# Attention and GEGLU block on one core: a raw copy for half products, dense loads placed after the last sums' store, and two-step cycles from step 24

## The chip, the cores and the metric

The kernel runs on 1 core of one Trainium2 chip. The metric is device time in microseconds (us) of that core, the median of several runs; lower is better. Engines are named as the profile names them: PE is TensorE's matmuls and PEld its weight loads, DVE is VectorE, ACT is ScalarE, POOL is GpSimd, SP is SyncE, which here only issues DMAs. A queue of DMAs belongs to the engine that issues them, and an engine issues them in its program order.

## The reference

One transformer block on 2048 tokens of width 512: attention with 32 query heads of 16 elements over one shared key and value head, then a GEGLU feed-forward layer of width 1792. Both have a layer norm ahead and a residual behind.

```python
def _A_ref(x, wq, wk, wv, wo):
    q = split_heads(x @ wq)            # 32 heads of 16
    k, v = x @ wk, x @ wv              # shared by all heads
    p = softmax((q @ k.T) * 16 ** -0.5)
    return merge_heads(p @ v) @ wo

def _B_ref(x, w_gate, w_up, w_down):
    return (gelu(x @ w_gate) * (x @ w_up)) @ w_down

h = x + _A_ref(layernorm(x), wq, wk, wv, wo)
out = h + _B_ref(layernorm(h), w_gate, w_up, w_down)
```

## The kernel before

**Tiling.** The tokens are cut into four query blocks b of 512 (`NB`, `T`). Attention goes block by block, in each block through eight groups g of four heads (`NG`), in each group through 16 chunks of 128 keys (`KC`). One step n is one key chunk for two of the four heads: two matmuls of scores into a tile `s` (L394), and one exponential of 128x1024 by ACT from `s` to `p` (L398). Two steps make a chunk, a group is 32 steps, a block 256. When a chunk's `p` is there, `weigh` multiplies it with the values and adds into the PSUM bank `acc` (L402). Chunks that are scored and not yet weighed stand in the list `pend`, and `finish(k)` weighs the oldest k of them. With a group's last chunk `evacuate` copies `acc` to `oT` (DVE, L415), stores it in DRAM as `acc_d` (SP, L419), reads it back re-ordered as `oc` (SP, L428), inverts the sums (L442), multiplies (L445) and splits the result in a high and a low part `o_hi` and `o_lo` (L453, L457). Two groups share one `oc`. When a block's groups are done, the output projection `pp` (L590), layer norm and feed-forward layer of that block (`dense(b)`, matmuls of L913 and L590) are woven into the scores of the next block.

**Products in two parts.** Matmul operands are split into a high and a low part, and a product is three matmuls per 128 rows (high x high, high x low, low x high). The query projection `pq` of a block is four such products, c = 0 to 3 (`project_q`). Its first products run whole (L204). From block 1, c = 2 on they are half products (L392): each matmul takes 64 of the 128 rows of the array, and a score matmul takes the other 64 at the same time. Such a matmul is a token that the generator yields; the loop over n hands tokens to `scores`. When a half product is complete, DVE splits it from its bank into `qh` and `ql` (L119, L120), squares `qh` to `qs` (L1091), and SP stores three parts into `q_d` (L245). After c = 3 the generator yields `REST` for a cycle without tokens, then the matmuls `pqn` (L256) add up the squares of the block's four products, and DVE and POOL make a bound for the softmax from it (`qn`, `mm`, `m`). All `pq` and `pqn` of this stage use one PSUM bank: the pool has one buffer (`width = 1`), and the next product starts when the bank's last reader is done. For three of the whole products, listed in `HURRY`, DVE or ACT copies the bank to a tile `pq_raw` first and the split reads that.

**The first block's loop.** It has two parts. The first, `while n < 2 * KC`, advances whole products at the steps of `RAMP` and then at every fourth step, until the generator yields 0 (`said`), and calls `finish(len(pend) - 2)` at every fourth step: the order on PE is four steps of scores, then two weighings. The second, `while n < lead`, runs cycles of two steps, weighs one chunk per cycle when more than two are pending, and gives out up to four tokens per cycle, later two (`count`). In between it calls `next(parts)`: that loads a piece of the dense weights on SP (L497), splits it on POOL, and stores it to DRAM from POOL's queue (L508, L514). `age()` counts down to the softmax bound's steps. At n = 256 the buffers of this phase are released and POOL loads the output weights `wo` (L564). Four steps later `dense(0)` is started, which issues the loads of two `xb` tiles (L624) and four `w` tiles (L550) on SP. At n = 272 the first block's output projection begins.

**The order.** PE, POOL, ACT, and from the first loop on SP and DVE, run exactly in the order in which the code records instructions. The attention code stands a second time in the program, in a branch that these inputs do not take.

Of the kernel before, what the change touches and what calls it, by code (L numbers as in the profile page):

```python
# [40 lines left out]
HURRY = ((0, 3), (1, 0), (1, 1))  # L41
# [11 lines left out]
def kernel(  # L53
# [26 lines left out]
    KC = S // P  # L80
# [77 lines left out]
    def run(outer, first):  # L158
# [28 lines left out]
        def project_q(b, cs, eng, col, whole=None):  # L187
            halves = whole is not None
            whole = whole if halves else cs
            tsl = slice(b * T, (b + 1) * T)  # L190
            xT_hi, xT_lo = xT[b]
            urgent = b == 0 and cs[0] == 0
            qss = []
            for c in cs:
                pq = psum1(f"pq_{b}_{c}")
                terms = [
                    (wt[:, d, c * P : (c + 1) * P], xt[:, d, :])
                    for d in range(DC)
                    for wt, xt in ((wq_hi, xT_hi), (wq_hi, xT_lo), (wq_lo, xT_hi))
                ]  # L200
                last = len(terms) - 1
                full = c in whole
                for n, (lhsT, rhs) in enumerate(terms if full else ()):
                    nc.tensor.matmul(pq, lhsT, rhs, start=(n == 0), stop=(n == last))  # L204
                    if n % 3 == 2 and (urgent or n < last):
                        yield 3
                for a in range(2) if not full else ():
                    if a:
                        mark = eb.tile([P, 1], F32, tag="qmark", bufs=2, name=f"mark_{b}_{c}")
                        nc.vector.tensor_copy(mark, pq[:, :1])  # L210
                    rows = slice(64 * a, 64 * a + 64)
                    for n, (lhsT, rhs) in enumerate(terms):
                        yield a, last - n, partial(
                            nc.tensor.matmul, pq, lhsT[rows], rhs[rows],
                            start=(a == 0 and n == 0), stop=(a == 1 and n == last),
                            skip_group_check=True,
                        )

                raw = None
                if (b, c) in HURRY:  # L220
                    raw = eb.tile([P, T], F32, tag="vT", bufs=3, name=f"pq_raw_{b}_{c}")
                    if b == 0:
                        nc.scalar.activation(raw, pq, AF.Copy)
                    else:
                        nc.vector.tensor_copy(raw, pq)
                    yield 3
                qh = eb.tile([P, T], F32R, tag="qh", bufs=2, name=f"qh_{b}_{c}")
                ql = eb.tile([P, T], F32R, tag="ql", bufs=2, name=f"ql_{b}_{c}")
                if raw is not None:
                    split(nc.vector, qh, ql, raw)  # L230
                else:

                    split(nc.vector if b == 0 and c == FIRST_Q else eng, qh, ql, pq)
                qs = eb.tile([P, T], BF16, tag="qs", bufs=DC, name=f"qs_{b}_{c}")
                square = partial(
                    (nc.gpsimd if urgent else nc.vector).tensor_tensor,
                    qs, qh.bitcast(F32), qh.bitcast(F32), op=ALU.mult,
                )
                if full:
                    square()  # L240
                else:
                    squares.append(square)
                qss.append(qs)
                for r0, part in ((0, qh), (DH, ql), (2 * DH, qh)):
                    nc.sync.dma_start(  # L245
                        q_d[c * HC : (c + 1) * HC, r0 : r0 + DH, tsl].bitcast(F32),
                        part.bitcast(F32),
                    )
                if not halves and (raw is None or b == 0):
                    yield 3  # L250

            if halves:
                yield REST
            pn = psum1(f"pqn_{b}_{cs[0]}")[:H, :]
            for i, c in enumerate(cs):
                nc.tensor.matmul(  # L256
                    pn, sel[:, c, :], qss[i], start=(i == 0), stop=(i == len(cs) - 1)
                )
            qn = eb.tile([H, T], F32, tag="qn", bufs=1, name=f"qn_{b}_{cs[0]}")
            nc.vector.tensor_copy(qn, pn)  # L260
            nc.vector.tensor_reduce(q2[:, col : col + 1], qn, axis=AX.X, op=ALU.max)

            mm = eb.tile([H, 3], F32, tag="mm", bufs=2, name=f"mm_{b}_{cs[0]}")

            def factors():
                nc.gpsimd.tensor_scalar(
                    mm[:, 0:1], q2[:, col : col + 1], k2m, 1e-30, op0=ALU.mult, op1=ALU.add
                )
                nc.gpsimd.tensor_tensor(
                    mm[:, 1:2], mm[:, 0:1], power[:H, 0:1], op=ALU.pow  # L270
                )
                nc.gpsimd.tensor_scalar(
                    mm[:, 2:3], mm[:, 0:1], mm[:, 1:2], 0.5, op0=ALU.mult, op1=ALU.mult
                )
                nc.gpsimd.tensor_scalar(
                    mm[:, 1:2], mm[:, 1:2], k2m, 0.5, op0=ALU.mult, op1=ALU.mult
                )

            m = eb.tile([H, T], F32R, tag="m", bufs=2, name=f"m_{b}_{cs[0]}")

            def bound():
                nc.vector.tensor_scalar(
                    m, qn, mm[:, 1:2], mm[:, 2:3], op0=ALU.mult, op1=ALU.add
                )
                hs = slice(cs[0] * HC, (cs[-1] + 1) * HC)
                nc.sync.dma_start(q_d[hs, 3 * DH, tsl].bitcast(F32), m[hs].bitcast(F32))

            if urgent:
                yield 2
                factors()  # L290
                nc.scalar.activation(
                    m, qn, AF.Identity, bias=mm[:, 2:3], scale=mm[:, 1:2]
                )
                ms[b] = m
                return
            after.extend([[2, factors], [4, bound]])
            if not halves:
                yield 2
# [680 lines left out]
        PER = NG * KC  # L979
# [58 lines left out]
        with tc.manual_schedule(engines={mybir.EngineType.SP, mybir.EngineType.DVE}):  # L1038
# [2 lines left out]
                work = later_q()  # L1041
                parts = part_weights(early.enter_context(tc.tile_pool(name="parts", bufs=1)))

            while n < 2 * KC:
                for _ in range(RAMP.get(n, n > 7 and n % 4 == 3) if said else 0):
                    said = next(work)
                    age()
                score(n)
                n += 1
                if n % 4 == 0:  # L1050
                    finish(len(pend) - 2)
                    if parts is not None and n > 12 and n % 24:
                        next(parts)

            token, left = next(work) if first else None, 6 * (NB * DC - 2 - DC) * DC
            while n < lead:
                age()
                rest = token == REST
                count = 0
                if token is not None and not rest:  # L1060
                    count = min(4 if left > LAST_Q - n else 2, token[1] + 1)
                    left -= count
                if n == 2 * PER:
                    assert token is None
                    while after:
                        age()
                    for _ in parts or ():
                        pass
                    if first:
                        check_bound(eb, k2m)  # L1070
                    parts = work = None
                    early.close()
                    db = late.enter_context(tc.tile_pool(name="dense", bufs=1))
                    load_wo(0)
                for j in range(2):
                    if j >= 2 - count // 2:
                        tokens = token, next(work)
                        score(n, [(lane, step) for lane, _, step in tokens])
                        token = next(work, None)
                    else:  # L1080
                        score(n)
                    n += 1
                if n == 2 * PER + 4:
                    primed = dense(0)
                    next(primed)
                if rest:
                    token = next(work, None)
                if len(pend) > 2:
                    finish(1)
                while squares:  # L1090
                    squares.pop(0)()  # L1091
                if outs and n % 4 == 0:
                    take_out()
                if parts is not None and n // 2 % 5 in (0, 2):
                    next(parts, None)
# [23 lines left out]
        for c in range(LEAD[0], (NB - 1) * NG * len(SIZES)):  # L1119
# [18 lines left out]
            due, said = 0, None  # L1138
# [380 lines left out]
```

## Time and profile before

| | before |
|---|---|
| median of 3 runs | 1426.1 us (1425.7 to 1427.6) |
| the profiled execution, its own time | 1426.9 us |
| its span, first to last instruction | 1425.1 us |
| PE busy | 1402.1 us, 98% |
| ACT busy | 1045.1 us, 73% |
| DVE busy | 541.8 us, 38% |
| POOL busy | 200.1 us, 14% |
| DMA | 193.69 MB, mean 136 GB/s |

Busy time of PE is a sum over matmuls whose ends are modelled, so 98% does not say that PE works at its peak. A row of the timeline has start, length, engine, line, operation, output<-input with shapes, and in brackets the idle time of that engine just before it, with what ended it. A row of the chain of waits has start, length and what the program's end depended on there. In rows of waits the three numbers are microseconds in total, how often, and the longest.

### The profile page before, as it was taken

What the parts mean: (1) busy time and instruction counts of PE and PEld (TensorE: products, weight loads), DVE (VectorE), ACT (ScalarE), POOL (GpSimd) and SP (SyncE); (2) the same over time, 40 slices, a digit from 0 to 9 for tenths busy, and PEclk for the clock granted to TensorE, in tenths of its full rate; (3) what the DMA queues carried; (4) which work ended last, traced back from release to release, by engine and by line L of the source; (5) the groups of instructions that cost most, each with busy time, mean ns of one, the idle gap of its engine ahead of it and who ended that gap; (6) DMA issues with size and microseconds to landing.
All of it is one profiled execution on the core that took longest, in us unless ns stands there. A gap on an engine that the chain in (4) does not pass through costs nothing.

```text
span 1425.1 us, 25577 instructions
## 1 busy us (share of the span) xinstructions
PE 1402.1 (98%) x10622; PEld 777.5 (55%) x10622; DVE 541.8 (38%) x974; ACT 1045.1 (73%) x1149; POOL 200.1 (14%) x286
## 2 busy tenths in 40 slices
PE   8999999998999999999999999999999999999998
PEld 7533333324555555555555555555555555557886
DVE  7412221213352342424352342423443342427665
ACT  7699999995787787877787777777778777772000
POOL 6365666620000000000000000000000000002000
PEclk9999999999999999999999999999999999999999
DMA  4467776761243241304242242223243241435551
GB/s 158 162 210 264 237 251 230 247 212 48 85 138 109 86 145 61 112 29 176 102 153 93 88 143 72 99 82 124 84 147 115 86 146 34 143 125 193 183 200 62
DMA packets 84700, 193.69 MB, mean 136 GB/s; under 512 B 9676, under 2 KB 24012, under 8 KB 84544
## 3 DMA queue, kind: packets, MB, share of 16 engines
q1 hardware_dynamic: 77208, 165.65, 35.3%
q0 software_dynamic: 7200, 26.22, 4.9%
q8 instruction: 85, 1.39, 0.4%
q14 instruction: 39, 0.32, 0.1%
q10 hardware_dynamic: 168, 0.10, 0.0%
HBM read 142.12 MB, written 49.55 MB: 134 GB/s over the span
## 4 chain that ended last, share of the span: by engine, by line
PE 91%; ACT 3%; DVE 2%; DMA 2%; issue 1%; SPq 0%; POOL 0%; DVEq 0%; ACTq 0%; POOLq 0%
PE acc L402 32%; PE s L394 20%; PE pu L913 9%; PE pg L913 7%; PE pd L913 4%; PE pd L590 3%; PE pd L612 3%; PE pg L612 3%; PE pu L612 3%; PE pq L392 2%; ACT p L398 2%; PE pp L590 2%; DMA acc_d<-oT 1%; PE pq L204 1%; PE pp L721 1%
## 5 line engine op out<-in xcount | busy, mean ns | idle before, releaser
L398 ACT ACTIVATE p<-s 128x1024 f32<-128x1024 f32 x1024 | 973.8, 1030 | 237.5 <-PE s L394 235.5
L402 PE MATMUL acc<-p,v_sb 128*32 128x512 f32 x4096 | 499.3, 601 | 0.0
L394 PE MATMUL s<-qg,kaug 50*128 50x512 f32 x1984 | 420.5, 427 | 3.5 <-ACT p L398 3.5
L394 PEld LDWEIGHTS s<-qg,kaug 50*128 50x128 f32 x1984 | 191.6, 184 | 254.5 <-ACT p L398 156.7
L402 PEld LDWEIGHTS acc<-p,v_sb 128*32 128x32 f32 x4096 | 107.9, 109 | 227.5 <-issue 222.4
L913 PE MATMUL pg<-x2h,w 64*128 64x512 f32 x672 | 211.7, 391 | 1.4 <-DVE h L855 0.7
L913 PE MATMUL pu<-x2h,w 64*128 64x512 f32 x672 | 212.3, 391 | 0.0
L913 PEld LDWEIGHTS pu<-x2h,w 64*128 64x128 f32 x672 | 115.8, 185 | 16.3
L913 PEld LDWEIGHTS pg<-x2h,w 64*128 64x128 f32 x672 | 116.1, 185 | 14.8 <-DVE mark_pg L936 1.6
L913 PE MATMUL pg<-x2l,w 64*128 64x512 f32 x336 | 122.0, 390 | 0.0
L913 PE MATMUL pu<-x2l,w 64*128 64x512 f32 x336 | 121.7, 390 | 0.0
L790 ACT ACTIVATE ga<-ga 128x512 f32<-128x512 f32 x56 | 35.3, 634 | 89.2 <-DVE ga L785 89.2
L129 POOL TENSOR_SCALAR rstd<-mv 128x1 f32<-128x1 f32 x16 | 3.6, 222 | 686.8 <-DVE mv L127 686.7
L913 PE MATMUL pd<-w,gh 64*128 64x512 f32 x384 | 81.2, 392 | 0.0
L855 DVE TENSOR_TENSOR h<-h,pd 128x512 f32<-128x512 f32 x48 | 31.9, 685 | 115.5 <-PE pd L913 66.4
L442 DVE RECIPROCAL oc<-oc 128x128 f32<-128x128 f32 x64 | 56.3, 921 | 33.9 <-DMA oc<-acc_d 29.2
L1146 DVE SCALAR_TENSOR_TENSOR ga<-ga,g 128x512 f32<-128x512 f32 x70 | 48.3, 691 | 52.7 <-ACT ga L790 51.7
L774 DVE COPY g<-pg 128x512 f32<-128x512 f32 x56 | 38.7, 691 | 62.8 <-PE pg L913 57.1
L913 PEld LDWEIGHTS pu<-x2l,w 64*128 64x128 f32 x336 | 57.9, 185 | 8.0
L913 PEld LDWEIGHTS pg<-x2l,w 64*128 64x128 f32 x336 | 58.0, 185 | 6.2
L415 DVE COPY oT<-acc 128x512 f32<-128x512 f32 x32 | 22.1, 692 | 100.4 <-PE acc L402 100.2
L787 DVE TENSOR_TENSOR g<-g,pu 128x512 f32<-128x512 f32 x56 | 38.4, 685 | 40.6 <-PE pu L913 30.6
(258 smaller groups left out, 1441.3 us busy)
## 6 DMA issues: line engine op xcount, KB each, us to landing
w<-w_d SPq DMA_DIRECT2D x112, 512.0 KB
w<-w_d SPq DMA_DIRECT2D x28, 1024.0 KB
qg<-q_d SPq DMA_DIRECT2D x48, 200.0 KB
q_d<-qh SPq DMA_DIRECT2D x32, 256.0 KB
acc_d<-oT SPq DMA_DIRECT2D x31, 256.0 KB
oc<-acc_d SPq DMA_DIRECT2D x124, 64.0 KB
w_d<-w_0b POOLq DMA_DIRECT2D x14, 512.0 KB, 5.9
w_d<-w_1b POOLq DMA_DIRECT2D x14, 512.0 KB, 5.8
```

What stands on the lines that cost most here:

```text
L394: nc.tensor.matmul(s[:, a, :], kaug[rows, kc * P : (kc + 1) * P], qg[rows, 2 * u + a, :], start=True, stop=True,)
L398: nc.scalar.activation(p[:, 2 * u : 2 * u + 2, :], s, AF.Exp, scale=SCALE)
L402: nc.tensor.matmul(acc[32 * j : 32 * j + 32, :], v_sb[:, kc, :], p[:, j, :], start=(kc == 0), stop=(kc == KC - 1), skip_group_check=True,)
L442: nc.vector.reciprocal(oc[:, 1, sl], oc[:, 1, sl])
L590: nc.tensor.matmul(banks[k], lhsT[rows], rhs[rows], start=(turn == 0 and i == 0), stop=(turn == 1 and i == n - 1), skip_group_check=True,)
L612: nc.tensor.matmul(bank, lhsT, rhs, start=(i == 0), stop=(i == len(ts) - 1))
L774: nc.vector.tensor_copy(g, pg)
L787: nc.vector.tensor_tensor(g, g, pu, op=ALU.mult)
L790: nc.scalar.activation(a, a, AF.Tanh, scale=GELU_A * GELU_C)
L855: nc.vector.tensor_tensor(hs[t], hs[t], pd, op=ALU.add)
L913: nc.tensor.matmul(e["bank"], lhsT[rows], rhs[rows], start=i == 0 and not e["both"], stop=last and e["both"], skip_group_check=True,)
L1146: (soon or lazy).pop(0)()
```

## The change

Three edits in one diff.

1. In `project_q`, a half product is copied to `pq_raw` by DVE too, and the split reads the copy. The whole products of `HURRY` stay as they were, and so does their pause (`yield 3`).
2. The loop's first part ends when the generator has yielded 0, not at n = 32. From there the second part's cycles run; tokens are not given out before n = 32.
3. `dense(0)` is started at n = 264 instead of n = 260.

```diff
-                if (b, c) in HURRY:
+                if (b, c) in HURRY or not full:
                     raw = eb.tile([P, T], F32, tag="vT", bufs=3, name=f"pq_raw_{b}_{c}")
                     if b == 0:
                         nc.scalar.activation(raw, pq, AF.Copy)
                     else:
                         nc.vector.tensor_copy(raw, pq)
-                    yield 3
+                    if full:
+                        yield 3
...
-            while n < 2 * KC:
+            while n < 2 * KC and said:
...
-                if token is not None and not rest:
+                if token is not None and not rest and n >= 2 * KC:
...
-                if n == 2 * PER + 4:
+                if n == 2 * PER + 8:
                     primed = dense(0)
                     next(primed)
```

Line numbers behind L228 are higher by one in the changed kernel, so L394 becomes L395, and L419 becomes L420.

PE, in group 0 of block 0, steps 24 to 31 (`s_0` and `s_1` are a chunk's two steps, two matmuls each; `acc` is one weighing, four matmuls; `pq` is block 1, c = 2). Before:

```order
L394 MATMUL s_0_1034<-qg_first,kaug 128x512 x2
L394 MATMUL s_1_1038<-qg_first,kaug 128x512 x2
L394 MATMUL s_0_1043<-qg_first,kaug 128x512 x2
L394 MATMUL s_1_1047<-qg_first,kaug 128x512 x2
L402 MATMUL acc_0_803<-p_1003,v_sb 32x512 x4
L402 MATMUL acc_0_803<-p_1012,v_sb 32x512 x4
L394 MATMUL s_0_1066<-qg_first,kaug 128x512 x2
L394 MATMUL s_1_1070<-qg_first,kaug 128x512 x2
L394 MATMUL s_0_1075<-qg_first,kaug 128x512 x2
L394 MATMUL s_1_1079<-qg_first,kaug 128x512 x2
L402 MATMUL acc_0_803<-p_1033,v_sb 32x512 x4
L402 MATMUL acc_0_803<-p_1042,v_sb 32x512 x4
```

The same place in the changed kernel:

```order
L395 MATMUL s_0_1044<-qg_first,kaug 128x512 x2
L395 MATMUL s_1_1048<-qg_first,kaug 128x512 x2
L403 MATMUL acc_0_803<-p_1003,v_sb 32x512 x4
L395 MATMUL s_0_1059<-qg_first,kaug 128x512 x2
L395 MATMUL s_1_1063<-qg_first,kaug 128x512 x2
L403 MATMUL acc_0_803<-p_1012,v_sb 32x512 x4
L395 MATMUL s_0_1072<-qg_first,kaug 128x512 x2
L395 MATMUL s_1_1076<-qg_first,kaug 128x512 x2
L403 MATMUL acc_0_803<-p_1043,v_sb 32x512 x4
L395 MATMUL s_0_1091<-qg_first,kaug 128x512 x2
L395 MATMUL s_1_1095<-qg_first,kaug 128x512 x2
L403 MATMUL acc_0_803<-p_1058,v_sb 32x512 x4
```

The same eight score rows and four weighings stand there; a weighing now follows every two steps. This is all that moves on PE ahead of the branch that is not taken.

SP, at the end of block 0 (`b_d` is the softmax bound's check; `acc_d<-oT_7` is the store of group 7; `oc_3` the reads of its sums; `qg_1` the next queries). Before:

```order
L1441 DMA b_d<-q2m 32x1
L624 DMA xb_0_3373<-in_A_x_dram 128x512
L624 DMA xb_1_3375<-in_A_x_dram 128x512
L550 DMA w_0_0_3379<-w_d 128x1024
L550 DMA w_0_1_3381<-w_d 128x1024
L550 DMA w_0_2_3383<-w_d 128x1024
L550 DMA w_0_3_3385<-w_d 128x1024
L419 DMA acc_d<-oT_7_3391 128x512
L428 DMA oc_3_3096<-acc_d 16x2x512 x4
L374 DMA qg_1_3405<-q_d 50x2x512 x2
```

In the changed kernel:

```order
L1442 DMA b_d<-q2m 32x1
L420 DMA acc_d<-oT_7_3397 128x512
L429 DMA oc_3_3107<-acc_d 16x2x512 x4
L375 DMA qg_1_3411<-q_d 50x2x512 x2
L625 DMA xb_0_3436<-in_A_x_dram 128x512
L625 DMA xb_1_3438<-in_A_x_dram 128x512
L551 DMA w_0_0_3442<-w_d 128x1024
L551 DMA w_0_1_3444<-w_d 128x1024
L551 DMA w_0_2_3446<-w_d 128x1024
L551 DMA w_0_3_3448<-w_d 128x1024
```

The six dense loads moved behind the store, the four reads and the two query loads. Elsewhere on SP and POOL the weights' pieces stand up to one piece later among the stores of `q_d` and the steps of the bound.

DVE, block 1, c = 2 and c = 3 (`mark` reads one column of the bank half way). Before:

```order
L210 COPY mark_2_1174<-pq_2_1106 128x1
L119 CAST qh_2_1233<-pq_2_1106 128x512
L120 TENSOR_TENSOR ql_2_1234<-pq_2_1106,qh_2_1233 128x512
L1091 TENSOR_TENSOR qs_2_1237<-qh_2_1233 128x512
L210 COPY mark_3_1301<-pq_3_1241 128x1
L119 CAST qh_3_1366<-pq_3_1241 128x512
L120 TENSOR_TENSOR ql_3_1367<-pq_3_1241,qh_3_1366 128x512
L1091 TENSOR_TENSOR qs_3_1370<-qh_3_1366 128x512
```

In the changed kernel:

```order
L210 COPY mark_2_1168<-pq_2_1042 128x1
L225 COPY pq_raw_2_1227<-pq_2_1042 128x512
L119 CAST qh_2_1229<-pq_raw_2_1227 128x512
L120 TENSOR_TENSOR ql_2_1230<-pq_raw_2_1227,qh_2_1229 128x512
L1092 TENSOR_TENSOR qs_2_1233<-qh_2_1229 128x512
L210 COPY mark_3_1296<-pq_3_1237 128x1
L225 COPY pq_raw_3_1362<-pq_3_1237 128x512
L119 CAST qh_3_1364<-pq_raw_3_1362 128x512
L120 TENSOR_TENSOR ql_3_1365<-pq_raw_3_1362,qh_3_1364 128x512
L1092 TENSOR_TENSOR qs_3_1368<-qh_3_1364 128x512
```

One copy stands ahead of each split, and the cast and the subtraction read `pq_raw` instead of the bank. It is so at all ten half products.

## The prediction

> **What bounds the kernel now.** I read the page's chain first, then the chain in order of time over the first query block (60 to 420 us), then the stretches where it leaves TensorE.
>
> ```profile
> PE 91%; ACT 3%; DVE 2%; DMA 2%; issue 1%; SPq 0%; POOL 0%; DVEq 0%; ACTq 0%; POOLq 0%
> ```
>
> TensorE sets the end nearly everywhere, so only time that TensorE gets back counts. All that the diff moves lies ahead of 345 us. There the chain leaves TensorE for long at one place:
>
> ```profile
> 308.37 0.70 DVE oT L415
> 309.09 9.94 DMA acc_d<-oT
> 320.35 2.26 DMA oc<-acc_d
> 322.79 3.40 DVE oc L442 x4
> 326.21 0.70 DVE oc L445
> 327.42 1.22 PE pp L590 x4
> ```
>
> The columns are start, length and what it is. This is group 7 of block 0: its sums go to DRAM (L419), come back re-ordered (L428), are divided, and the output projection `pp` needs them. The store takes 9.94 us. Stretches of the same place (length; busy time of PE, PEld, DVE, ACT, POOL; granted clock; DMA share; GB/s):
>
> ```profile
> 302.00:309.00 7.00, 7.00 (x48) 1.96 (x40) 0.63 (x1) 7.00 (x9) 1.50 (x2) 1.00 0.85 265
> 309.00:317.00 8.00, 8.00 (x58) 2.28 (x56) 0.06 (x1) 8.00 (x10) 0.00 (x0) 1.00 0.95 382
> 317.00:323.90 6.90, 5.91 (x46) 3.19 (x38) 1.11 (x2) 5.94 (x7) 0.00 (x0) 1.00 0.36 106
> 323.90:327.40 3.50, 0.23 (x2) 0.00 (x0) 3.40 (x6) 1.33 (x2) 0.00 (x0) 0.89 0.04 10
> 327.40:333.40 6.00, 5.98 (x30) 2.42 (x34) 0.85 (x2) 1.94 (x2) 0.00 (x0) 0.50 0.00 0
> 333.40:340.00 6.60, 6.60 (x62) 3.71 (x58) 0.79 (x2) 4.14 (x5) 0.00 (x0) 0.99 0.01 2
> ```
>
> While the store is under way the DMA engines are full (0.95). Then TensorE stands for 3.5 us, and afterwards works 6.0 us at a granted clock of 0.50, which makes 3.0 us of work into 6.0. So the late sums cost 3.5 + 3.0 = 6.5 us.
>
> **Part 1: the dense loads behind the store.** What fills the engines:
>
> ```profile
> 302.10 1.51 POOL L564 DMA_DIRECT2D wo<-wo_d  x2 [7.44 <-PE s L394]
> ...
> 302.47 1.86 SPq L550 DMA_DIRECT2D w<-w_d  x4
> ...
> 319.04 1.73 SPq L428 DMA_DIRECT2D oc<-acc_d  x4
> ...
> SPq L428 <- DMA acc_d<-oT: 70.0, 31, 9.6
> ```
>
> On SP's queue two `xb` (256 KB each) and four `w` (512 KB each, page part 6) stand ahead of the 256 KB store: 2.5 MB. POOL's queue brings 2 MB of `wo` at the same time. In the new order SP issues store, four reads `oc`, two `qg`, and only then `xb` and `w`. Nothing is added; six DMAs move past seven.
>
> How long will the store take now? The 30 other stores kept SP waiting (70.0 - 9.6) / 30 = 2.0 us on average, and one among the weights' traffic:
>
> ```profile
> 248.66 0.65 SPq L419 DMA_DIRECT2D acc_d<-oT  x1
> 255.18 1.77 SPq L428 DMA_DIRECT2D oc<-acc_d  x4
> ```
>
> 6.5 us. Between these ends I take 3.5, since the 2 MB of `wo` alone, from 302.1 at the 265 GB/s of the row above, are gone by about 310. From the reads' issue to the first reciprocal were 322.79 - 319.04 = 3.75 us, from there to `pp` 327.42 - 322.79 = 4.63. In the times of the old run `pp` can then go at 309.09 + 3.5 + 3.75 + 4.63 = 321.0 (319.5 to 324.0 for the two ends), and TensorE asks for it at 323.9. The stall goes, at the worst end just so. The cover is 2.9 us; what it hides is this chain. Gone with the stall is its cold clock.
>
> The Trainium skill, "TensorE: Matmul & The Clock Gate", section "What's actually happening", says that an idle window of about 3.4 us halves the clock and a busy one of about the same length restores it. The trace agrees on the drop (3.5 us idle, then 0.50) but shows 6.0 us at half, not 3.4; by the page's window the cold part would be an estimated 1.7 us and this term 5.2 instead of 6.3. The trace decides.
>
> I take 6.3 of the 6.5, leaving 0.2 for a short wait on the exponentials, which have less lead when TensorE runs on; bounds 5.8 and 6.6. Who waits for the loads that are now late? After a store at 309.09, 3.5 us and the issue of six reads they leave near 315, about 12.5 us later: 2.5 MB at 265 to 382 GB/s take 7 to 9 us. First users:
>
> ```profile
> 339.21 1.29 DVE L645 TENSOR_TENSOR h<-pp,xb 128x512 f32<-128x512 f32 x2 [9.45 <-PE pp L590]
> ...
> L913 PEld LDWEIGHTS pg<-x2h,w x28: 183/186/188, 363.7 to 379.9; 64*128 64x128 f32 x28
> ```
>
> `xb` is asked for at 339.2 - 6.3 = 332.9 and is there near 319; `w` at 363.7 - 6.3 = 357.4 and there near 324. Cost nothing, with 14 us of cover or more.
>
> **Part 2: the raw copy.** Ten half products (blocks 1 to 3) get one more DVE copy each, 0.69 us, and the bank is free after it instead of after `qh` and `ql`. Block 2, c = 1:
>
> ```profile
> 149.91 1.06 PE L402 MATMUL acc<-p,v_sb 128*32 128x512 f32 x8
> 150.01 0.69 DVE L119 CAST qh<-pq 128x512 fp32r<-128x512 f32 x1 [7.71 <-PE pq L392]
> 150.74 0.69 DVE L120 TENSOR_TENSOR ql<-pq,qh 128x512 fp32r<-128x512 f32 x1
> ...
> 151.48 0.18 PEld L392 LDWEIGHTS pq<-xT_hi,wq_hi 64*128 64x128 f32 x1 [0.40 <-DVE ql L120]
> ...
> 152.15 1.06 PE L402 MATMUL acc<-p,v_sb 128*32 128x512 f32 x8
> ...
> 154.04 1.07 PE L402 MATMUL acc<-p,v_sb 128*32 128x512 f32 x8
> ...
> PEld pq L392 <- DVE ql L120: 3.8, 7, 1.4
> ```
>
> The cycle with the hand-over takes 152.15 - 149.91 = 2.24 us, the next 1.89: 0.35 lost, because the next product starts its bank only after `ql`. With the copy the bank is free at about 150.7, ahead of the scores that TensorE runs first. The last row (all such waits: total, count, longest) is one of 1.41 and six of 0.40. The six give 6 x 0.35 = 2.1. The long one (block 1, c = 2) stops the scores behind it too: ScalarE then waits 0.77 instead of the 0.19 of a usual cycle,
>
> ```profile
> 96.25 1.94 ACT L398 ACTIVATE p<-s 128x1024 f32<-128x1024 f32 x2 [0.19 <-PE s L394]
> 98.95 1.94 ACT L398 ACTIVATE p<-s 128x1024 f32<-128x1024 f32 x2 [0.77 <-PE s L394]
> ```
>
> 0.58 more. Together 2.7 at most; I take 2.5, bounds 2.1 and 2.7.
>
> Against it stands c = 3, three times. There the next thing on TensorE is `pqn`, the sum of squares, which needs `qs`, and `qs` comes after the added copy:
>
> ```profile
> 197.48 0.68 DVE L1091 TENSOR_TENSOR qs<-qh 128x512 bf16<-128x512 f32 x1
> ...
> 198.36 0.38 PE L256 MATMUL pqn<-qs,sel 128*32 128x512 bf16 x1
> ...
> 71.94 0.40 DVE L119 CAST qh<-pq_raw 128x512 fp32r<-128x512 f32 x1
> 72.38 0.69 DVE L120 TENSOR_TENSOR ql<-pq_raw,qh 128x512 fp32r<-128x512 f32 x1
> ...
> L453 DVE CAST o_hi<-oc x15: 416/426/1010, 153.0 to 1222.0; 128x512 fp32r<-128x512 f32 x15
> L457 DVE TENSOR_TENSOR o_lo<-oc,o_hi x15: 684/691/1662, 153.5 to 1226.6; 128x512 fp32r<-128x512 f32 x15
> ...
> 100.00:294.00 194.00, 122.50 (x142) 1.00 0.75 243
> ```
>
> `pqn` already starts just after `qs` ends (198.16), so every delay of `qs` is TensorE's. The copy adds 0.72 (start to start), and the cast from SBUF is shorter, 0.44 instead of 0.73 start to start: +0.43. But casts and subtractions with SBUF operands alone have lasted up to 1.01 and 1.66 us (min/median/max in the rows of L453 and L457), so the other end is 0.43 + 0.58 + 0.97 = 2.0. The medians lie at the short end; I take 0.65 each, 3 x 0.65 = +1.95, bounds +1.3 and +3.0 for the forecast, +6.0 in a rival.
>
> The Trainium skill, "SBUF — State Buffer", section "Who interferes with whom", speaks against this edit: VectorE shares a port pair with GpSimd when it copies within SBUF in its fast mode, or reads two SBUF operands, and the later of the two waits for the whole instruction. By it `qh` and `ql`, which read PSUM before, now can wait behind GpSimd's weight preparation; with GpSimd busy 122.50 of 194 us in 142 instructions of 0.86 us (last row), the estimate is 0.63 x 0.43 = 0.27 of waiting on each of the two, which makes the term 3 x (0.43 + 0.54) = +2.9 and the gain 0.95 smaller. The stretched maxima above agree with it; no run here shows how often it strikes.
>
> The seven other added copies hide behind TensorE's next twelve cycles of 1.89 us, in which nothing asks for `qs`; uncovered they would cost 0.43 each. Weight preparation on POOL and its loads on SP come up to one step later. POOL had idled 7.44 us before it issued `wo` (row above), so that costs nothing; without that cover it would be a step of up to four of POOL's instructions, 4 x 0.86 = 3.4 us.
>
> **Part 3: group 0.** Steps 24 to 31 are issued as four cycles of two scores and one weighing instead of two of four and two.
>
> ```profile
> 77.45 3.77 ACT L398 ACTIVATE p<-s 128x1024 f32<-128x1024 f32 x4 [0.22 <-PE s L394]
> ...
> 85.62 1.94 ACT L398 ACTIVATE p<-s 128x1024 f32<-128x1024 f32 x2 [0.42 <-PE s L394]
> ...
> 301.04 21.29 ACT L398 ACTIVATE p<-s 128x1024 f32<-128x1024 f32 x23
> ```
>
> Before, these eight took 85.62 - 77.45 = 8.17 us. The last row is a stretch that already runs such cycles without projection terms: 21.29 / 23 = 0.926 each, without a gap. Eight take 7.41: -0.76. The first cycle with terms, which TensorE bounds, also starts with more lead, so I take -0.9, bounds -0.6 and -1.3.
>
> **The sum**: -0.9 - 2.5 + 1.95 - 6.3 = -7.75. The profiled execution's own time is 1426.9 us, 1.8 more than its span, and 0.8 above the median of 1426.1. So 1426.9 - 7.75 = 1419.1 for such an execution, and **1418.3 us** for a median.
>
> **Rivals.** (a) The store stays late: if `wo` alone holds it for 9.9 us as before, the stall remains and only -1.45 is left: 1424.6. For it: it is not shown that SP's own 2.5 MB delayed it. Against it: the slowest of the seven stores before it took 6.5 us, among loads of the weights. (b) The copies cost more than they free: each `qs` at c = 3 is 2.0 late, +6.0: -0.9 - 2.5 + 6.0 - 6.3 = -3.7, 1422.4. For it the two maxima, against it both medians. (c) Slower: the dense loads come too late. They queue on SP behind reads that wait for the store. Should `w` land after 357.4, TensorE stands at the first `pg`, and the cold clock follows; 4.8 us of waiting plus 3.0 us of cold work make good the 7.8, and from `w` landing at 362 on the kernel is slower: at 366, 1426.1 + 4 = 1430. That would be 47 us after issue; in the old order the engines had emptied by about 319 (the DMA share falls to 0.36), 17 us after issue. It is nearly excluded.
>
> **Chances.** Forecast 0.74, (a) 0.10, (b) 0.12, (c) 0.04. The forecast's own range is the sum of the bounds: -1.3 - 2.7 + 1.3 - 6.6 = -9.3 to -0.6 - 2.1 + 3.0 - 5.8 = -5.5, 1416.8 to 1420.6. To hold 8 in 10 it reaches over (b): 1416.3 to 1422.5. About 0.2%, 2.9 us, is what a measurement can tell from no change. The forecast and nearly all of (b) are faster by more, 0.85; (a) is within, with the edge of (b), 0.11; slower 0.04.
>
> **What would show it.** Right: SP's wait between L420 and L429 of the last group near 3.5 us; no idle TensorE and no clock below 1.00 around 322 to 333; the waits of `pq` for `ql` gone from the list and none on `pq_raw` of 0.3 or more; `pqn` at c = 3 about 0.65 later behind its product; the eight exponentials of steps 24 to 31 in one row without a gap. Wrong: a store of over 7 us; a cold stretch left, or a new one near the first `h<-pp,xb` or `pg`; casts from `pq_raw` at 0.7 us and more as a rule; ScalarE gaps of 1.2 us and more at each c = 3.

## The result and the profile after

| | before | changed |
|---|---|---|
| median, measured together | 1425.55 us (22 runs, 1420.03 to 1428.91) | 1421.88 us (22 runs, 1419.63 to 1429.27) |
| ratio | | 0.9983, 95% interval 0.9971 to 0.9996 |
| the profiled execution, span | 1425.1 us | 1418.9 us |
| first `h<-pp,xb` of block 0 | 339.21 us | 334.63 us |

By the ratio the change gains 0.17%, 2.4 us (the medians in the table lie 3.7 apart), which by the prediction's own bound of 0.2% is within what counts as no change; the forecast was 7.75 us. The two profiled executions differ by 6.2 us, nearly the forecast, but they are a longer one of the kernel before and a shorter one of the changed kernel (1420.61 us). So there are two questions: which terms of the sum came out otherwise in this pair, and why the repeated times show less than the pair.

**Late sums.** The chain of the changed kernel at the end of block 0 (start, length, what):

```profile
309.59 0.70 DVE oT L416
...
310.30 6.78 DMA acc_d<-oT
...
325.68 0.73 PE pp L591 x4
```

The stretches there (length; PE, PEld, DVE, ACT, POOL busy; clock; DMA share; GB/s), and in the timeline the last weight piece and the first step of the softmax bound `mm` on POOL, the bound's check `b_d`, `wo` and TensorE's wait:

```profile
323.90:327.40 3.50, 3.17 (x28) 1.91 (x28) 2.50 (x5) 2.60 (x3) 0.00 (x0) 1.00 0.99 397
327.40:333.40 6.00, 6.00 (x56) 3.09 (x50) 0.00 (x0) 3.45 (x5) 0.00 (x0) 1.00 0.30 117
```

```profile
298.39 1.29 POOL L120 TENSOR_TENSOR w213b<-w213r,w213b 128x512 fp32r<-128x512 f32 x1
...
299.78 0.26 POOL L267 TENSOR_SCALAR mm<-q,k2m 32x1 f32<-32x1 f32 x1
...
302.44 0.36 SPq L1442 DMA_DIRECT2D b_d<-q2m  x1
...
307.90 1.45 POOL L565 DMA_DIRECT2D wo<-wo_d  x2 [5.82 <-DMA b_d<-q2m]
...
325.68 0.73 PE L591 MATMUL pp<-wo,o_hi 64*128 64x512 f32 x4 [0.33 <-DVE o_hi L454]
```

Before, `mm` began 6.7 us earlier, after a wait for VectorE:

```profile
293.04 0.25 POOL L266 TENSOR_SCALAR mm<-q,k2m 32x1 f32<-32x1 f32 x1 [2.66 <-DVE q L261]
```

The stall is 0.33 us instead of 3.29 and the clock stays at 1.00. But the store took 6.78 us, not 3.5: GpSimd came to `wo` at 307.90 instead of 302.10, just ahead of the store at 310.30. Group 7's `oT` stands 1.22 us later than before and the first `h` 4.58 earlier: this stage gained 5.8.

**Group 0 and the banks.** Rows of ACT, changed and then before:

```profile
77.43 11.11 ACT L399 ACTIVATE p<-s 128x1024 f32<-128x1024 f32 x12 [0.21 <-PE s L395]
88.70 1.94 ACT L399 ACTIVATE p<-s 128x1024 f32<-128x1024 f32 x2 [0.16 <-PE s L395]
...
107.86 3.83 ACT L399 ACTIVATE p<-s 128x1024 f32<-128x1024 f32 x4 [0.18 <-PE s L395]
113.20 1.94 ACT L399 ACTIVATE p<-s 128x1024 f32<-128x1024 f32 x2 [1.50 <-PE s L395]
```

```profile
89.87 1.94 ACT L398 ACTIVATE p<-s 128x1024 f32<-128x1024 f32 x2 [0.18 <-PE s L394]
...
109.61 3.83 ACT L398 ACTIVATE p<-s 128x1024 f32<-128x1024 f32 x4 [0.18 <-PE s L394]
114.22 1.94 ACT L398 ACTIVATE p<-s 128x1024 f32<-128x1024 f32 x2 [0.78 <-PE s L394]
```

Twelve exponentials run without a gap from 77.43: the thirteenth starts at 88.70 instead of 89.87, and with the 0.02 that the first started earlier, part 3 is worth -1.15. At 107.86 against 109.61 it is -1.75; the other -0.6 is the long wait of block 1, c = 2. The next rows, at c = 3, show the opposite: a gap of 1.50 instead of 0.78. The half products' ends, changed and before (150.01 is quoted above):

```profile
125.91 0.69 DVE L225 COPY pq_raw<-pq 128x512 f32<-128x512 f32 x1 [2.08 <-PE pq L393]
148.62 0.69 DVE L225 COPY pq_raw<-pq 128x512 f32<-128x512 f32 x1 [7.70 <-PE pq L393]
173.41 0.69 DVE L225 COPY pq_raw<-pq 128x512 f32<-128x512 f32 x1 [11.20 <-PE pq L393]
196.11 0.69 DVE L225 COPY pq_raw<-pq 128x512 f32<-128x512 f32 x1 [9.64 <-PE pq L393]
```

```profile
126.94 0.69 DVE L119 CAST qh<-pq 128x512 fp32r<-128x512 f32 x1 [2.08 <-PE pq L392]
...
173.08 0.69 DVE L119 CAST qh<-pq 128x512 fp32r<-128x512 f32 x1 [11.21 <-PE pq L392]
196.15 0.69 DVE L119 CAST qh<-pq 128x512 fp32r<-128x512 f32 x1 [9.65 <-PE pq L392]
```

The changed kernel's lead is 1.03, then 1.39, then -0.33, then 0.04. A plain hand-over gains 0.36 (22.71 us instead of 23.07), as forecast. The third step lost 1.72, so 2.08 us went somewhere that the prediction did not name. The later ACT gaps, changed and before:

```profile
157.85 41.69 ACT L399 ACTIVATE p<-s 128x1024 f32<-128x1024 f32 x44 [2.03 <-PE s L395]
201.41 13.29 ACT L399 ACTIVATE p<-s 128x1024 f32<-128x1024 f32 x14 [1.86 <-PE s L395]
...
294.12 29.44 ACT L399 ACTIVATE p<-s 128x1024 f32<-128x1024 f32 x32 [1.83 <-PE s L395]
```

```profile
200.36 13.30 ACT L398 ACTIVATE p<-s 128x1024 f32<-128x1024 f32 x14 [0.78 <-PE s L394]
...
292.89 29.44 ACT L398 ACTIVATE p<-s 128x1024 f32<-128x1024 f32 x32 [0.55 <-PE s L394]
```

At the three c = 3 the gaps grew by 0.72, 1.08 and 1.28, 3.08 in all in this pair, where 1.95 was forecast. The new stall before 157.85, with the timeline ahead of it:

```profile
149.34 1.47 DVE L119 CAST qh<-pq_raw 128x512 fp32r<-128x512 f32 x1
...
151.45 1.19 DVE L1092 TENSOR_TENSOR qs<-qh 128x512 bf16<-128x512 f32 x1
...
152.16 1.61 POOL L120 TENSOR_TENSOR w_0b<-w_0r,w_0b 128x512 fp32r<-128x512 f32 x1
...
152.56 1.77 DVE L446 TENSOR_TENSOR oc<-oc 128x512 f32<-128x512 f32 x1
...
155.52 0.68 DVE L416 COPY oT<-acc 128x512 f32<-128x512 f32 x1
...
156.26 1.06 PE L403 MATMUL acc<-p,v_sb 128*32 128x512 f32 x8 [2.00 <-DVE oT L416]
```

VectorE's queue holds the split of block 2, c = 1, then the last multiplication of groups 0 and 1, then `oT` of group 2 (counted from 0 as above; the expectations below call it group 3), which frees `acc`. Everything there is stretched, and `oT` comes 2.00 us after TensorE asks. Before, the same row waits for TensorE:

```profile
155.18 0.69 DVE L415 COPY oT<-acc 128x512 f32<-128x512 f32 x1 [0.71 <-PE acc L402]
```

So there was 0.71 of slack on VectorE at that place, and the added copy plus the stretching used it up.

The pair's sum up to group 7's `oT`: -1.15 - 0.6 - 6 x 0.36 + 3.08 + 2.08 = +1.25, against +1.22 read off; the -5.8 behind it is itself read off. The other 1.6 of the 6.2 arises behind the first `h`, where the diff moves nothing; four executions of before (three of them below) differ by 1.2 in that stretch.

### The profile page after: what moved, and what is told of

It reads as the page before. It is cut to its first block, busy times and chain, and to the rows that moved or that the text cites. A ratio compares the mean times of both kernels' runs of the same rounds, so it can differ in the third digit from the quotient of the medians.

```text
span 1418.9 us, 25587 instructions
## 1 busy us (share of the span) xinstructions
PE 1397.5 (98%) x10622; PEld 776.7 (55%) x10622; DVE 551.5 (39%) x984; ACT 1044.2 (74%) x1149; POOL 202.9 (14%) x286
## 3 DMA queue, kind: packets, MB, share of 16 engines
q8 instruction: 85, 1.39, 0.4%
## 4 chain that ended last, share of the span: by engine, by line
PE 91%; ACT 3%; DVE 3%; DMA 2%; issue 1%; POOL 0%; SPq 0%; DVEq 0%; ACTq 0%; POOLq 0%
PE acc L403 32%; PE s L395 20%; PE pu L914 9%; PE pg L914 7%; PE pd L914 4%; PE pd L591 3%; PE pd L613 3%; PE pg L613 3%; PE pu L613 3%; ACT p L399 2%; PE pq L393 2%; PE pp L591 2%; PE pq L204 1%; PE pp L722 1%; DMA w_1r<-in_B_w_up_dram 1%
## 5 line engine op out<-in xcount | busy, mean ns | idle before, releaser
L395 PE MATMUL s<-qg,kaug 50*128 50x512 f32 x1984 | 418.8, 426 | 3.5 <-ACT p L399 3.5
L395 PEld LDWEIGHTS s<-qg,kaug 50*128 50x128 f32 x1984 | 191.5, 184 | 254.8 <-ACT p L399 155.4
```

The costliest lines, as they stand in the source:

```text
L395: nc.tensor.matmul(s[:, a, :], kaug[rows, kc * P : (kc + 1) * P], qg[rows, 2 * u + a, :], start=True, stop=True,)
```

## The experiments

### What the kernel before does in its other executions

Of 102 times of the kernel before, taken beside these runs, 34 lie at 1420.0 to 1422.4 us and 54 at 1424.5 to 1429.2, the rest between. The first three, on which the prediction stood, all lay in the upper group. Three more profiles, kernel unchanged:

> The kernel before, unchanged, to catch an execution of the shorter kind (its times lie in two groups, near 1421 and near 1427 us). Theory: the store of block 0's last sums lands only when the dense loads and `wo` (4.6 MB) are through, 15 to 17.4 us after their issue, and whether TensorE then stands for about 3.5 us and goes on at half clock (3 us more), or hardly waits, hangs on 1 or 2 us in that. In an execution near 1421 the store then takes 8.5 us or less (9.94 in the first profile), TensorE waits under 1 us before the output projection's first matmul, and the clock stays at 1.00 from 322 to 334. In one near 1427 all is as in the first profile. Rival: the two groups come from elsewhere, and an execution near 1421 shows the stall and the cold clock too, and is short in other stages.

> The kernel before once more, for the same question. Theory: an execution near 1421 us has no stall before the output projection and no granted clock of 0.50 near 327; one near 1427 has both. Rival: both kinds have both.

> The kernel before once more, for the same question. Theory: an execution near 1421 us has no stall before the output projection and no granted clock of 0.50 near 327; one near 1427 has both. Rival: both kinds have both.

Their times were 1426.47, 1420.97 and 1423.2 us, one of each kind. The first repeats the old picture (store 10.09 us, stall 3.38). The second, at 1420.97, its store from the chain and the two stretches:

```profile
310.44 6.38 DMA acc_d<-oT
```

```profile
323.90:327.40 3.50, 3.33 (x28) 2.15 (x28) 1.99 (x5) 2.77 (x4) 0.00 (x0) 1.00 0.00 0
327.40:333.40 6.00, 6.00 (x56) 3.11 (x50) 0.00 (x0) 3.19 (x5) 0.00 (x0) 1.00 0.00 0
```

The third, at 1423.2: its store from the chain, TensorE's wait in the timeline, and the stretch of 6 us that was at half clock in the first profile.

```profile
309.75 9.09 DMA acc_d<-oT
```

```profile
327.23 0.73 PE L590 MATMUL pp<-wo,o_hi 64*128 64x512 f32 x4 [2.45 <-DVE o_hi L453]
```

```profile
327.40:333.40 6.00, 6.00 (x52) 2.58 (x54) 0.66 (x2) 2.54 (x3) 0.00 (x0) 1.00 0.00 0
```

The theory holds for the stall and the clock. The store landed at 316.83 in the second execution and at 318.86 to 319.19 in the other three, 14.7 and 16.6 to 16.9 us after the issue of `wo`. The early landing leaves no stall, the late ones leave 2.45 to 3.38, and only the longer ones (3.29 and 3.38) are followed by half clock. But the landing is not all of it. Group 7's `oT` stands at 309.72 in the second execution, 1.35 us later than in the first profile, so TensorE asked for the sums later too. What made it late is the square `qs` at c = 3 of blocks 1 and 3, which reads two operands from SBUF. Two gaps of ACT in this execution, and the square ahead of the second (0.68 us in the first profile):

```profile
114.88 1.94 ACT L398 ACTIVATE p<-s 128x1024 f32<-128x1024 f32 x2 [1.50 <-PE s L394]
...
290.89 1.54 DVE L1091 TENSOR_TENSOR qs<-qh 128x512 bf16<-128x512 f32 x1
...
294.25 29.44 ACT L398 ACTIVATE p<-s 128x1024 f32<-128x1024 f32 x32 [1.27 <-PE s L394]
```

In the first profile these gaps are 0.78 and 0.55. So gaps like those of the changed kernel occur without any copy.

The stall follows from the time between the start of `oT` and the landing: 10.67, 10.83 and 9.83 us in the three executions with a stall, 7.11 in the one without. In all seven profiles of this document that have such a stall, of whichever kernel, that time less the stall is 7.2 to 7.5 us. That is the work that TensorE has in between. As long as the landing stays where it is, time lost ahead of `oT` only shortens a stall that is there, and time won ahead of it lengthens it.

The first `h` stands at 334.62, 336.24 and 339.22 us in the second, third and first of the three, and 1085 us (1084.7 to 1085.6) follow in each: the spread of the kernel's times is made ahead of it. So, by the times, the 6.3 us to be won are there in about half of the executions, and a third have nothing of them. Why the 4.5 MB took 2 us less in one was not settled.

### Each edit alone, and two of them

The kernel before with one edit: the copies; the cycles; the later dense loads. The fourth is the changed kernel with this line put back and its pause as before:

```diff
-                if (b, c) in HURRY or not full:
+                if (b, c) in HURRY:
```

> Edit 1 alone. My theory after the changed kernel's trace (VectorE's reads of two SBUF operands and its SBUF casts wait for GpSimd's whole instructions): six banks win 0.35 us each and the seventh 0.58, the three pqn lose 0.7 to 1.3 each (+3.1), and the chain of stretched DVE work ahead of group 3's oT may cost up to 2.1 more; block 0 ends 0.4 to 2.5 us later, the cold stretch after the late sums stays, the time is 0 to 3 us above the kernel before. Rival (the copies are as I predicted, medians): -2.5 + 1.95, 0.5 us below it.

> Edit 2 alone. Theory: steps 24 to 31 run without a gap and the first half product starts about 1.2 us earlier; the weights' pieces on POOL end later, so that the load of wo is issued near 306 us or later instead of 302. With the dense loads still ahead of the store the late sums stay as costly as before: 1.2 us faster. Rival (the later wo load delays the output projection by itself): the stall grows and the time is 0 to 3 us above the kernel before.

> Edit 3 alone. Theory: wo is loaded from 302 us as before, the store has no dense loads ahead of it and lands in 3 to 5 us (it took 6.8 in the changed kernel, where wo started at 308), no stall and no cold clock: 6.3 us faster than an execution of the kernel before that has the stall. Rival (SP's loads were not what delayed the store): the store takes over 6 us here too.

> Edits 2 and 3 without the raw copy. Theory: against the changed kernel it loses the 2.7 us of the banks and wins the 3.1 of the three pqn and the 2.1 ahead of group 3's oT: 2.5 us faster than the changed kernel, 7 faster than an execution of the kernel before that has the stall. Rival (the copies pay as predicted): 0.5 us slower than the changed kernel.

| | median, us | range | ratio to before | interval |
|---|---|---|---|---|
| before (35 runs) | 1423.89 | 1420.18 to 1429.2 | | |
| copies alone | 1426.29 | 1421.29 to 1429.1 | 1.0019 | 1.0003 to 1.0035 |
| cycles alone | 1428.68 | 1425.72 to 1430.17 | 1.0032 | 1.002 to 1.0045 |
| loads alone | 1420.21 | 1419.29 to 1421.79 | 0.9972 | 0.996 to 0.9983 |
| cycles and loads, no copies | 1419.52 | 1418.85 to 1420.37 | 0.997 | 0.9958 to 0.9982 |

**Loads alone** takes the upper group of times away and leaves the lower one where it was. `wo`, the store and the reads of its profile:

```profile
303.37 1.51 POOL L564 DMA_DIRECT2D wo<-wo_d  x2 [8.28 <-DMA b_d<-q2m]
...
309.52 0.34 SPq L419 DMA_DIRECT2D acc_d<-oT  x1
312.41 1.72 SPq L428 DMA_DIRECT2D oc<-acc_d  x4
```

2.89 us from store to reads, near the 3.5 of the forecast, with `wo` 6 us ahead. In all eight profiles with the dense loads behind the store, here and below, it landed 8.7 to 9.7 us after `wo` was issued, and its own time, 2.1 to 7.6 us, hung on how far ahead `wo` had left (7.1 to 1.7 us). With the dense loads in front, six profiles, it landed 14.6 to 16.9 us after `wo`. Loads alone is worth 0.28%, 4.0 us by the ratio, where the term said 6.3. **Copies alone** costs 2.7 (0.19%); the prediction's own terms for it sum to -0.55. Its profile is of one of its shortest executions (1421.61 us, `oT` at 310.16, no stall), so where the median of 1426.29 loses its time is not shown. **Cycles alone** is slower by 4.6, where 1.2 faster was expected and the rival had 0 to 3 slower: its profile has group 7's `oT` 0.3 us earlier, but the dense loads leave at 304.93 instead of 301.59, so the store lands later. The store, and TensorE's wait:

```profile
308.79 13.17 DMA acc_d<-oT
```

```profile
330.31 1.22 PE L590 MATMUL pp<-wo,o_hi 64*128 64x512 f32 x4 [6.41 <-DVE o_hi L453]
```

It landed 16.6 us after `wo` was issued at 305.42, about the lag of three of the four profiles of before. The granted clock was 0.50 behind this stall too, for 6 us. With the dense loads behind the store this loss is gone (last row of the table). **Without the copies** the kernel is 2.4 us faster than the changed one by the medians, 1.9 by the ratios to before.

### GpSimd as the cause of the stretched splits

The changed kernel without GpSimd's split of the feed-forward weights: it reads one column of each piece, and a constant tile goes to DRAM in its place, so this kernel leaves the real weights of the feed-forward layer out.

```diff
-                both = pw.tile([P, 2, D], F32R, tag="w_both", bufs=2, name=f"{name}b")
-                if halve:
-                    nc.gpsimd.tensor_scalar(raw, raw, 0.5, None, op0=ALU.mult)
-                split(nc.gpsimd, both[:, 0], both[:, 1], raw, nc.gpsimd)
-                return both
+                seen = pw.tile([P, 1], F32, tag="w_seen", bufs=2, name=f"{name}s")
+                nc.gpsimd.tensor_copy(seen, raw[:, :1])
+                return same
```

> The changed kernel without GpSimd's split of the dense weights: GpSimd touches one column of each loaded piece, and the stores send one constant tile, so DMA traffic stays and GpSimd's work on 512 columns is gone (the feed-forward layer's weights are not the reference's). Theory (VectorE's casts and two-operand reads within SBUF wait for GpSimd): every cast qh<-pq_raw takes 0.40 to 0.45 us, every ql and qs 0.69, the three waits of pqn for qs shrink from 0.7-1.3 to about 0.45 over the kernel before, group 3's oT is on time, block 0 ends 3.5 us earlier than in the changed kernel. Rival (DMA traffic into SBUF stretches them): casts still reach 1 us and more, and the stall before group 4 may stay.

1417.48 us (1416.46 to 1419.1), ratio 0.9948 (0.9933 to 0.9964). The ten splits of this kernel and then of the changed one (min/median/max in ns):

```profile
L119 DVE CAST qh<-pq_raw x10: 426/427/428, 96.3 to 286.4; 128x512 fp32r<-128x512 f32 x10
...
L120 DVE TENSOR_TENSOR ql<-pq_raw,qh x10: 692/693/695, 96.7 to 286.9; 128x512 fp32r<-128x512 f32 x10
```

```profile
L119 DVE CAST qh<-pq_raw x10: 426/608/1465, 96.2 to 289.6; 128x512 fp32r<-128x512 f32 x10
...
L120 DVE TENSOR_TENSOR ql<-pq_raw,qh x10: 691/693/1648, 97.1 to 290.1; 128x512 fp32r<-128x512 f32 x10
```

Without GpSimd's work beside it every split lasts the same. From 100 to 294 us GpSimd is busy 32 us instead of 118, while the DMA engines are as full as in the changed kernel (0.76 against 0.74), so it is GpSimd and not the DMAs. The gaps at c = 3 are 1.11, 1.11 and 0.87, each 0.33 above the first profile of before: 1.0 us of the pair's 3.08 is the copy itself, 2.1 is waiting. The stall on group 2's `oT` is gone. This agrees with the Trainium skill, "SBUF — State Buffer", section "Who interferes with whom": VectorE and GpSimd share a port pair, whoever holds it blocks the other, and an operation with one operand in SBUF in its plain mode is free of it. The copies from the bank stayed at 0.69 us throughout.

### Where the copy pays

Four variants of the changed kernel: the square ahead of `ql` at c = 3; copies only for c below 3; copies there except block 2, c = 1, and the weights' pieces at their old steps; all copies, with the pieces at their old steps. The second's line, then the third's two (the fourth has the last alone):

```diff
-                if (b, c) in HURRY or not full:
+                if (b, c) in HURRY or not full and c < DC - 1:
```

```diff
-                if (b, c) in HURRY or not full:
+                if (b, c) in HURRY or not full and c < DC - 1 and (b, c) != (2, 1):
...
-                if parts is not None and n // 2 % 5 in (0, 2):
+                if parts is not None and (n % 4 == 0 if n <= 2 * KC else n // 2 % 5 in (0, 2)):
```

> The changed kernel, with the square qs ahead of ql at c = 3. Theory: qs is ready 0.7 us earlier, with contention on the cast alone; the three gaps of ScalarE fall from 1.5-1.9 to 0.5-1.1, 2 us faster than the changed kernel. Rival (the gap comes from the bank's chain pqn, qn and not from qs): no change.

> The changed kernel with the raw copy at c = 0, 1, 2 only. Theory: the pqn are as early as without copies, six banks still win 0.35 and one 0.58; the stall ahead of group 3's oT may stay: 3.1 us faster than the changed kernel, 0.6 us faster than edits 2 and 3 without any copy if that stall (2.1) is there, 2.7 if not. Rival: no faster than without copies by over 0.5, if stretched DVE work shows up elsewhere.

> As the last, with no copy at block 2, c = 1 either, and with the weights' pieces kept at the steps they had in the kernel before. Theory: no late oT, wo loaded near 302 and the store landing in 3 us, as with edit 3 alone: 2.3 us faster than edits 2 and 3 without copies, near 1417.2 us. Rival (the copies' gain is lost again behind ScalarE, which is nearly full there): within 0.7 us of edits 2 and 3 without copies.

> All three edits, but the dense weights' pieces stay at their old steps (28 and 32 as counted before), so GpSimd's preparation and `wo` are no step later. Theory: `wo` is issued near 302 instead of 307.9, the store of the last sums takes 2 to 4 us instead of 6.8, and no execution is left near 1428; the costs at c = 3 and of group 3's late sums stay, so the time is 1420 to 1421, 1 us under the changed kernel. Rival: GpSimd's lateness only used up slack, the time is the changed kernel's within 0.5 us. If instead the pieces' steps decide how GpSimd's work meets VectorE's splits, the gaps at c = 3 change by more than 0.5 us each and the time can move to either side by 2 us.

| | median, us | ratio to before | interval |
|---|---|---|---|
| square first | 1421.06 | 0.998 | 0.9965 to 0.9995 |
| copies for c below 3 | 1420.57 | 0.9981 | 0.9967 to 0.9995 |
| the same without block 2, c = 1, pieces kept | 1417.55 | 0.9949 | 0.9931 to 0.9967 |
| all copies, pieces kept | 1421.4 | 0.9975 | 0.9963 to 0.9988 |

**Square first** is a miss: 0.8 us faster by the medians where 2 were expected; in its profile, of its longest execution, the gaps at c = 3 are 1.90, 1.63 and 1.22, and the one behind group 2's late `oT` is 3.35 us. Another order on VectorE did not take the splits out of GpSimd's way. **Copies for c below 3** is 1.3 faster by the medians where 3.1 were expected. It brings ACT's gaps at c = 3 back to 0.79, 0.92 and 0.55, but keeps the late `oT` (a gap of 2.02), and its store took 7.07. **The third** takes the copy of block 2, c = 1 away too, and no such gap is left; at c = 3 of block 1, where it has no copy, a gap of 1.46 is, as in the second execution of before. The splits of its profile, both kinds side by side (min/median/max in ns):

```profile
L119 DVE CAST qh<-pq_raw x6: 426/427/1093, 96.2 to 264.1; 128x512 fp32r<-128x512 f32 x6
L119 DVE CAST qh<-pq x4: 692/692/693, 108.3 to 286.1; 128x512 fp32r<-128x512 f32 x4
...
L120 DVE TENSOR_TENSOR ql<-pq_raw,qh x6: 693/1010/1664, 96.7 to 264.5; 128x512 fp32r<-128x512 f32 x6
L120 DVE TENSOR_TENSOR ql<-pq,qh x4: 691/692/692, 109.0 to 286.8; 128x512 fp32r<-128x512 f32 x4
```

What reads the bank keeps to 0.69; what reads SBUF alone stretches up to 1.66. Between 90 and 315 us no gap of ACT other than the three at c = 3 is above 0.45. This variant beats both kernels: 7.3 us below before by the ratio (4.7 to 9.8), 4.3 below the changed one by the medians. **All copies, pieces kept** has `wo` at 303.26 and the store from 309.60 to 312.29, 2.7 us; the time is 0.5 below the changed kernel by the medians (1.1 by the ratios), within what the two intervals leave open. The gap behind the late `oT` is 1.44 there, so it is the copy and not the pieces' steps that makes it. None of its 12 times is above 1423.6, where the changed kernel had two of 22 above 1428; that GpSimd's lateness made those two is likely but not shown, since neither was profiled.

## Why the prediction was wrong

Two steps failed: the worth of the late sums for a median, and the seven copies that were to hide. The first leaves 2.3 us of the forecast 7.75 unearned, the second 2.1.

**Part 1, the late sums: the mechanism right, the worth on the median too large.** "Gone with the stall is its cold clock" holds in the pair of profiles (5.8, bounds 5.8 and 6.6). The step that failed is the last one, "So 1426.9 - 7.75 = 1419.1 for such an execution, and **1418.3 us** for a median": it took one execution's stall for every execution's. With the loads edit alone the average worth is 4.0. The three times at hand, all within 2 us, gave no sign of that, and one profile shows one execution only: where `oT` was 1.35 us later and the store landed 2.2 us earlier, no stall was left to win.

**"3.5" for the store, "costs nothing" for the pieces moved a step later:** 6.78 measured, because `wo` left at 307.90. The 7.44 us that GpSimd idled ahead of `wo` were a wait for the end of the old buffers' phase, not spare time ahead of everything that GpSimd does: the softmax bound `mm` stood behind the last weight piece, and `wo` behind the bound's check. With the pieces at their old steps `wo` was back at 303.26. The forecast survived on its cover, with 0.33 of stall.

**Part 2, the seven other copies: the failed claim.** They "hide behind TensorE's next twelve cycles of 1.89 us, in which nothing asks for `qs`". Nothing asks for `qs`, but `oT` of group 2 is behind it in VectorE's queue, with 0.71 us to spare in the first profile and 0.28 to 0.74 in the others of before, and TensorE needs it to free `acc`: +2.08 in the pair. All five profiles with this copy beside GpSimd's work have the gap (1.44 to 3.35), and none of the others has it.

**Part 2, c = 3: the place right, the size open between the forecast and the pair.** +1.95 forecast, +3.08 in the pair. But the first profile of before has no long `qs` at c = 3, and two of the other three have. Over all profiles the three gaps sum to 4.5 to 5.2 us with the copy (three profiles, not counting the reordered one and the one without GpSimd's work) and to 2.1 to 3.6 without it (nine): on average +2.3, inside the forecast's +1.3 to +3.0. "The medians lie at the short end" weighed all 15 splits of `oc` across the program, 12 of which come after 300 us, where GpSimd is busy 2% of the time instead of 63%; the +2.9 that the prediction estimated beside it errs to the other side.

**Parts that held:** the six plain hand-overs (0.36 each, forecast 0.35), the long one (0.6, forecast 0.58), group 0 (-1.15, inside -0.6 to -1.3), and the dense loads with cover to spare (the first `h` does not wait for `xb`).

With the measured terms: -1.15 - 2.76 + 3.08 + 2.08 - 4.0 = -2.75, or -3.5 with the 2.3, against the measured -2.4 (-4.1 to -0.6). For no copies they give -5.15 (measured -4.3), and for the fastest variant (six copies: -0.6 - 5 x 0.36) -1.15 - 2.4 - 4.0 = -7.55, measured -7.3. For copies for c below 3 they give -5.83, and -2.7 was measured; that does not fit, and its stretched store is a likely part, but that was not tried by itself. Where the loads stay in front of the store the terms cannot be added, since time lost or won ahead of `oT` first changes the stall: that copies alone comes near (+2.4, measured +2.7) proves nothing, and cycles alone has the wrong sign.

The changed kernel's own median, 1421.88, lies 3.6 above the forecast 1418.3, and the short executions of the kernel before cannot explain that. The copies explain most: 2.1 at group 2 and 0.4 to 1.1 at c = 3.

Of the rivals, (a) had one thing right: the store still lands with `wo`, 9.2 us after its issue. But without the dense loads that was early enough, and the stall is gone. (b) had the time within 0.5 us, in part by luck: it put +6.0 at c = 3, where 2.3 to 3.1 arose, and did not name the place of the rest. (c) did not occur.

## What to carry to other kernels

A stall behind a transfer that lands just in time is a threshold, so one profile shows one side of it: read what 2 us more or less would do, on either side of the wait, and take several executions before its price enters a sum. To free a PSUM bank sooner by a copy to SBUF moves the work behind it from PSUM operands to SBUF operands, and so into GpSimd's way; spend the copy only where the queue behind it has slack, and look for that slack at the next instruction on the same engine that TensorE needs, not at the reader of the copy's result. Idle time ahead of an instruction counts as cover only if it is the same wait that a later start would still meet.

## What the runs showed of the hardware

- A stall of TensorE of 2.45 us left the granted clock at 1.00; stalls of 3.29, 3.38 and 6.41 were each followed by 6 us at about half. The short wait thus cost itself, those near 3.3 nearly double.
- With GpSimd at work a cast between SBUF tiles lasted 0.43 to 1.47 us and a subtraction 0.69 to 1.65; with its work left out all ten lasted the same to 3 ns. Splits that read the bank stayed at 0.69. The squares, with both operands in SBUF, stretch in the kernel before as well (0.68 to 1.56 us at c = 3).
- A 256 KB store issued 3 to 9 us behind 4.5 MB of loads landed 14.6 to 16.9 us after `wo`'s issue (six profiles); 1.7 to 7.1 us behind `wo`'s 2 MB alone it landed 8.7 to 9.7 us after `wo`'s issue (eight), whenever it was itself issued.
